# Expert logits from one side-by-side operand: eight matmuls a token tile instead of twelve

## The chip, the cores and the metric

The kernel runs on one core of a Trainium2 chip. The core has TensorE (PE; its weight loads are listed as PEld), VectorE (DVE), ScalarE (ACT), GpSimd (POOL) and SyncE (SP, which issues most DMA transfers; its queue is listed as SPq). The metric is device time in microseconds (us), lower is better. Before the change the median of 3 runs is 1145.32 us (1145.3 to 1145.65).

## What is computed

The reference chains three parts. Cut to what matters:

```python
# 1. attention between 512 tokens and 32 state rows, 8 batches x 8 heads, both ways -> 4352 tokens x 512
# 2. first MLP
h = x @ w_in                       # 512 -> 2048
x = np.maximum(h, 0.0) ** 2 @ w_out
# 3. one of 8 experts a token
xn = x / (np.linalg.norm(x, axis=-1, keepdims=True) + 1e-06)
en = expert_emb / (np.linalg.norm(expert_emb, axis=-1, keepdims=True) + 1e-06)
logits = xn @ en.T / tau
expert_idx = np.argmax(logits, axis=1)
gate_w = softmax(logits)[token, expert_idx]
out[mask] = gate_w * (np.maximum(x[mask] @ w1[e], 0.0) @ w2[e])   # for each expert e
```

## The kernel before

All matmuls work on 16-bit floats. To keep the precision of 32 bits, each operand is a pair of 16-bit halves, high and low, and each product is three matmuls: high by high, high by low, low by high.

The tokens are 34 tiles of 128. The first MLP takes two tiles (256 tokens) at a time, called u = 0 to 16: `up1` makes the hidden layer in 8 chunks (L1167 to L1169, or L1174 to L1176 for the last u, whose tokens come from the state side), `hidden` squares the ReLU on ScalarE (L1130, L1136) and splits it on VectorE into g_h and g_l (L1139, L1141), and `down1` multiplies by w_out (L1219 to L1221, four groups of 12 matmuls a tile). Each tile then goes through `route_tile`: ScalarE squares it for the norm (L1006), VectorE makes a scale, ScalarE and VectorE split it into halves (L308, L303), SP issues a DMA that transposes the halves into the tile xr (L1017), TensorE makes the 8 logits from xr and the expert embeddings (L1025 to L1028), and VectorE copies them out of PSUM (L1031). There is one buffer for xr. Four tiles together go through `route_group` (L1052 to L1105), a chain of small VectorE instructions that picks the expert, counts tokens and writes records to memory.

Beside this, `experts` prepares the expert weights: each is loaded in 1 MB pieces (stage, xx, wo_t), squared on ScalarE (L936), summed on VectorE (L872) and on TensorE by one small matmul (L878) for its scale, then converted into halves (L308 on ScalarE, L303 on VectorE, into he) and stored to w_d in memory (L325). There are 64 conversions of 1024 columns and two stores each. When all are stored, four 2 MB loads (L1436) bring the first experts' halves back; they also need the list of which expert comes first (`list_of`, whose small matmuls are L1255 and L1343). The expert MLP then runs 70 half steps on gathered tokens (L1527 to L1529, L1552).

Each engine runs its instructions in the order in which the program lists them. That order is made when the program is built, by the class `Plan`: each piece of work is a generator that yields an engine and a booked duration, and the planner lets the piece go next whose start is earliest, with a priority to break ties. A booking on TensorE for k matmuls of n columns is `pe(k, n)`: k times the larger of 4 ns and n x 0.4163 ns. A changed booking thus can change who goes next everywhere behind it. The order is fixed by then: where the chip's times differ from the bookings, nothing is corrected.

Of the kernel before, what the change touches and what calls it, by code (L numbers as in the profile page):

```python
# [11 lines left out]
F16 = mybir.dt.float16  # L12
# [3 lines left out]
ALU = mybir.AluOpType  # L16
X = mybir.AxisListType.X
# [5 lines left out]
NE, FE = 8, 1024  # L23
# [187 lines left out]
def act(n):  # L211
    return "act", 0.1 + 0.83e-3 * n
# [10 lines left out]
def tiny(k):  # L223
    return "dve", TINY * k


def pe(k, n):
    return "pe", k * max(0.004, n * 0.4163e-3)
# [3 lines left out]
def moe_kernel(  # L232
# [24 lines left out]
    const = ctx.enter_context(tc.tile_pool(name="const", bufs=1))  # L257
# [18 lines left out]
    mm = nc.tensor.matmul  # L276
    V = nc.vector
# [3 lines left out]
    def pow2(s, inv, v, K):  # L281

        m = small.tile([128, 4], F32, name="p2m")[:, :v.shape[1]]
        V.tensor_scalar(out=m.bitcast(I32), in0=v.bitcast(I32), scalar1=0x7F000000, scalar2=1,
                        op0=ALU.bitwise_and, op1=ALU.logical_shift_right)
        V.tensor_scalar(out=s.bitcast(I32), in0=m.bitcast(I32), scalar1=-1.0, scalar2=float(K << 23),
                        op0=ALU.mult, op1=ALU.add)
        V.tensor_scalar(out=inv.bitcast(I32), in0=m.bitcast(I32), scalar1=float((254 - K) << 23), scalar2=None,
                        op0=ALU.add)
# [15 lines left out]
    def split(hi, lo, src, scale, n):  # L305

        yield act(n)
        nc.scalar.activation(out=hi, in_=src, func=AF.Copy, scale=scale)  # L308
        yield dve(n)
        split_lo(lo, src, scale, hi)  # L310
# [46 lines left out]
    ise = const.tile([128, 2 * NE], F32, name="ise")  # L357
    u1 = const.tile([128, NT], F32, name="u1")
    itau = const.tile([128, 1], F32, name="itau")
    en_h = const.tile([128, 4, NE], F16, name="en_h")  # L360
    en_l = const.tile([128, 4, NE], F16, name="en_l")
    cum = const.tile([128, NT + 1, NE], F16, name="cum")
    nc.gpsimd.memset(cum[:, 0, :], 0.0)

# [15 lines left out]
    def ev(*key):  # L380
        return evs.setdefault(key, Ev(plan))
# [619 lines left out]
    def route_tile(i, ps, k_h, rc, st):  # L1001

        j = i % 4
        rc = rc.bitcast(F16)
        yield act(600)
        nc.scalar.activation(out=rc[:, 0:512].bitcast(BF16), in_=ps, func=AF.Square, accum_out=st["f2"][:, j:j + 1])  # L1006
        yield tiny(4)
        f2 = st["f2"][:, j:j + 1]
        V.tensor_scalar(out=f2, in0=f2, scalar1=FLOOR, scalar2=None, op0=ALU.max)  # L1009
        s2 = small.tile([128, 1], F32, name="s2")  # L1010
        pow2(s2, st["is2"][:, j:j + 1], f2, 204)
        yield from split(rc[:, 0:512], rc[:, 512:1024], ps, s2, 600)
        d_slots.release(k_h)
        yield xr_slots
        yield "sp", 0.06
        xr = mg.tile([128, 8, 128], F16, name="xr", bufs=XR)
        nc.sync.dma_start_transpose(xr, rc[:, 0:1024])  # L1017
        plan.cur[2] = plan.dma(1 << 18) + 1.0
        yield ev("en")
        at = plan.now()  # L1020
        yield t_slots
        plan.cur[2] = max(at, plan.now())
        pl = ps_t.tile([128, 512], F32, name="t")
        yield pe(12, NE)
        for k in range(4):  # L1025
            mm(pl[:, 0:NE], lhsT=xr[:, k, :], rhs=en_h[:, k, :], start=k == 0, stop=False)
            mm(pl[:, 0:NE], lhsT=xr[:, k, :], rhs=en_l[:, k, :], start=False, stop=False)
            mm(pl[:, 0:NE], lhsT=xr[:, 4 + k, :], rhs=en_h[:, k, :], start=False, stop=k == 3)  # L1028
        xr_slots.release()
        yield tiny(1)  # L1030
        V.tensor_copy(st["lg"][:, j, :], pl[:, 0:NE])  # L1031
        t_slots.release()
        ev("lg", i).set()

# [149 lines left out]
    def down1():  # L1184
        for u in range(NU):
            g = u // 2
            for j in range(2):
# [35 lines left out]
                if i % 4 == 0:  # L1223
                    plan.add(group_unscale(g), 1)
                plan.add(route_tile(i, ps, k_h, recs[-1], st), 2 if g < B else 0)
                if i % 4 == m - 1:
                    plan.add(route_group(4 * g, m, recs, k_r, st), 2 if g < B else 0)
# [447 lines left out]
```

## Time and profile before

| what | value |
|---|---|
| median of 3 runs | 1145.32 us |
| the profiled execution | 1157.43 us |
| its span, first to last instruction | 1155.6 us |
| mean granted TensorE clock | 0.959 of full speed |
| PE busy | 1032.8 us, 89% |
| DVE busy | 708.0 us, 61% |
| ACT busy | 583.3 us, 50% |
| POOL busy | 126.2 us, 11% |

The span is the time from the first to the last instruction of one profiled execution. Busy shares are averages over stages that differ: the page's second part cuts the span into 40 slices of 28.9 us, with one digit for tenths busy.

```profile
PE   2255899999999999999999999699999999999995
DVE  6998877968869878688696784356422222222221
ACT  6689777776776977677777873111111111101110
PEclk8579799999999999999999999899999999999998
```

The first four slices load weights and start the attention, the 25th and 26th are the passage from the first MLP to the expert MLP.

### The profile page before, as it was taken

What the parts mean: (1) busy time and instruction counts of PE and PEld (TensorE: products, weight loads), DVE (VectorE), ACT (ScalarE), POOL (GpSimd) and SP (SyncE); (2) the same over time, 40 slices, a digit from 0 to 9 for tenths busy, and PEclk for the clock granted to TensorE, in tenths of its full rate; (3) what the DMA queues carried; (4) which work ended last, traced back from release to release, by engine and by line L of the source; (5) the groups of instructions that cost most, each with busy time, mean ns of one, the idle gap of its engine ahead of it and who ended that gap; (6) DMA issues with size and microseconds to landing.
All of it is one profiled execution on the core that took longest, in us unless ns stands there. A gap on an engine that the chain in (4) does not pass through costs nothing. (4 is left out here: it accounts for less than half of the span.)

```text
span 1155.6 us, 26458 instructions
## 1 busy us (share of the span) xinstructions
PE 1032.8 (89%) x10707; PEld 665.2 (58%) x10707; DVE 708.0 (61%) x1838; ACT 583.3 (50%) x959; POOL 126.2 (11%) x149
## 2 busy tenths in 40 slices
PE   2255899999999999999999999699999999999995
PEld 1134356555555555565555666377776777767773
DVE  6998877968869878688696784356422222222221
ACT  6689777776776977677777873111111111101110
POOL 0200000200100201002001010212121211211201
PEclk8579799999999999999999999899999999999998
DMA  9345466566685685656736676634696777685690
GB/s 354 112 151 128 151 159 211 105 193 145 183 223 125 209 238 157 189 117 183 238 71 229 205 232 273 167 92 93 209 297 173 204 213 206 185 250 155 179 295 28
DMA packets 160546, 211.77 MB, mean 183 GB/s; under 512 B 112226, under 2 KB 113506, under 8 KB 155171
## 3 DMA queue, kind: packets, MB, share of 16 engines
q1 hardware_dynamic: 152098, 182.94, 55.5%
q0 software_dynamic: 8320, 27.08, 7.2%
q8 instruction: 86, 1.41, 0.5%
q14 instruction: 42, 0.34, 0.1%
HBM read 257.92 MB, written 51.68 MB: 268 GB/s over the span
## 5 line engine op out<-in xcount | busy, mean ns | idle before, releaser
L1219 PE MATMUL d<-wo_t,g_h 128*128 128x512 f16 x544 | 209.7, 386 | 3.6 <-DVE g_h L1139 1.4
L1221 PE MATMUL d<-wo_t,g_l 128*128 128x512 f16 x544 | 209.3, 385 | 1.8 <-DVE l L1063 1.8
L1220 PE MATMUL d<-wo_t,g_h 128*128 128x512 f16 x544 | 209.5, 385 | 1.2 <-DVE wo_t L303 1.2
L1486 ACT ACTIVATE r<-u 128x512 f32<-128x512 f32 x70 | 41.8, 597 | 324.5 <-PE u L1529 300.0
L1167 PE MATMUL u<-aT,sw 128*128 128x256 f16 x512 | 141.5, 276 | 25.3 <-ACT r L1130 22.5
L1169 PE MATMUL u<-aT,sw 128*128 128x256 f16 x512 | 141.4, 276 | 0.9 <-DVE sw L303 0.9
L1168 PE MATMUL u<-aT,sw 128*128 128x256 f16 x512 | 141.3, 276 | 0.0
L1130 ACT ACTIVATE r<-u,cg 128x512 f32<-128x512 f32 x136 | 93.0, 684 | 72.9 <-PE u L1176 35.4
L1489 DVE CAST hh<-r 128x512 f16<-128x512 f32 x70 | 30.4, 434 | 136.5 <-ACT r L1486 134.4
L1105 POOL DMA_INDIRECT rec_d<-rec,pi x34 | 37.8, 1112 | 576.6 <-DVE f L1009 175.7
L1141 DVE TENSOR_TENSOR g_l<-r,g_h 128x512 f16<-128x512 f32 x136 | 93.3, 687 | 6.5 <-ACT r L1136 5.1
L1500 DVE TENSOR_SCALAR o<-d,rec,wo_t 128x512 f32<-128x512 f32 x35 | 28.3, 810 | 108.9 <-PE d L1552 99.2
L1221 PEld LDWEIGHTS <-g_l 128*128 128x128 f16 x544 | 53.9, 99 | 70.2 <-issue 5.3
L1552 PEld LDWEIGHTS <-hh 128*128 128x128 f16 (+1 forms) x688 | 54.7, 102 | 56.9 <-issue 0.4
L1136 ACT ACTIVATE r<-r 128x512 f32<-128x512 f32 x136 | 85.6, 629 | 1.9
L1219 PEld LDWEIGHTS <-g_h 128*128 128x128 f16 x544 | 54.2, 100 | 55.9 <-issue 5.7
L1220 PEld LDWEIGHTS <-g_h 128*128 128x128 f16 x544 | 53.8, 99 | 53.5 <-issue 5.0
L1139 DVE CAST g_h<-r 128x512 f16<-128x512 f32 x120 | 50.9, 424 | 47.8 <-ACT r L1136 44.7
L1527 PE MATMUL u<-xes,stage 128*128 128x128 f16 x448 | 75.9, 219 | 0.0
L1529 PE MATMUL u<-xes,stage 128*128 128x128 f16 x448 | 75.9, 219 | 0.0
L1528 PE MATMUL u<-xes,stage 128*128 128x128 f16 x448 | 75.9, 219 | 0.0
L1168 PEld LDWEIGHTS <-sw 128*128 128x128 f16 x512 | 50.6, 99 | 37.6 <-issue 26.5
(334 smaller groups left out, 2682.3 us busy)
## 6 DMA issues: line engine op xcount, KB each, us to landing
w_d<-he SPq DMA_DIRECT2D x128, 256.0 KB
wo_t<-w_d SPq DMA_DIRECT2D x16, 2048.0 KB
stage<-w_d SPq DMA_DIRECT2D x14, 2048.0 KB
he<-w_d SPq DMA_DIRECT2D x14, 2048.0 KB
xx<-w_d SPq DMA_DIRECT2D x13, 2048.0 KB
sw<-w_d SPq DMA_DIRECT2D x13, 2048.0 KB
stage<-in_w_dram SPq DMA_DIRECT2D x20, 1024.0 KB
g_h<-w_d SPq DMA_DIRECT2D x8, 2048.0 KB
```

Of the source, the lines that this page charges most:

```text
L1130: nc.scalar.activation(out=r, in_=ps, func=AF.Relu, scale=cg[:, g:g + 1])
L1136: nc.scalar.activation(out=r, in_=r, func=AF.Square)
L1141: V.tensor_tensor(out=gl, in0=r, in1=gh, op=ALU.subtract)
L1167: mm(o, lhsT=hl[:, i, 0, fs], rhs=aT[:, i, :], start=i == 0, stop=False)
L1168: mm(o, lhsT=hl[:, i, 0, fs], rhs=aT[:, 2 + i, :], start=False, stop=False)
L1169: mm(o, lhsT=hl[:, i, 1, fs], rhs=aT[:, i, :], start=False, stop=i == 1)
L1219: mm(ps, lhsT=g_h[:, f, ts], rhs=w[:, 0, :], start=f == 0, stop=False)
L1220: mm(ps, lhsT=g_h[:, f, ts], rhs=w[:, 1, :], start=False, stop=False)
L1221: mm(ps, lhsT=g_l[:, f, ts], rhs=w[:, 0, :], start=False, stop=f == KF - 1)
L1527: mm(p[:, j, xs], lhsT=w[:, 0, k, fs], rhs=xe[:, k, xs], start=k == 0, stop=False)
L1528: mm(p[:, j, xs], lhsT=w[:, 0, k, fs], rhs=xe[:, 4 + k, xs], start=False, stop=False)
L1529: mm(p[:, j, xs], lhsT=w[:, 1, k, fs], rhs=xe[:, k, xs], start=False, stop=k == 3)
```

## The change

The two halves of the expert embeddings, 8 columns each, are put into one tile of 16 columns. The high half of the tokens is multiplied by all 16 at once; the low half of the tokens by the first 8 as before. Two sums of 8 columns stand in PSUM, and the instruction that takes them out adds them: a reduction over two elements in place of a copy. The booking for the planner falls from 12 matmuls to 8.

```diff
-    en_h = const.tile([128, 4, NE], F16, name="en_h")
-    en_l = const.tile([128, 4, NE], F16, name="en_l")
+    en = const.tile([128, 4, 2 * NE], F16, name="en")
+    en_h, en_l = en[:, :, 0:NE], en[:, :, NE:2 * NE]
...
         pl = ps_t.tile([128, 512], F32, name="t")
-        yield pe(12, NE)
+        yield pe(8, NE)
         for k in range(4):
-            mm(pl[:, 0:NE], lhsT=xr[:, k, :], rhs=en_h[:, k, :], start=k == 0, stop=False)
-            mm(pl[:, 0:NE], lhsT=xr[:, k, :], rhs=en_l[:, k, :], start=False, stop=False)
+            mm(pl[:, 0:2 * NE], lhsT=xr[:, k, :], rhs=en[:, k, :], start=k == 0, stop=False)
             mm(pl[:, 0:NE], lhsT=xr[:, 4 + k, :], rhs=en_h[:, k, :], start=False, stop=k == 3)
         xr_slots.release()
         yield tiny(1)
-        V.tensor_copy(st["lg"][:, j, :], pl[:, 0:NE])
+        V.tensor_reduce(out=st["lg"][:, j, :], in_=pl[:, 0:2 * NE].rearrange("p (a e) -> p e a", a=2), axis=X, op=ALU.add)
```

From the logits on, all line numbers of the changed kernel are smaller by one (L1130 of before is L1129, and so on). The order of instructions changes on all engines. Three places follow.

On ScalarE, at the end of the expert conversions (L308 into he): in the program before, the square of the 31st tile (L1006) stands ahead of the last conversion.

```order
L308 ACTIVATE he<-xx,se 128x1024 x2
L1130 ACTIVATE r<-u,cg 128x512
L1136 ACTIVATE r<-r 128x512
L1006 ACTIVATE rec_8505,f_8056<-d 128x512
L308 ACTIVATE he<-xx,se 128x1024
L308 ACTIVATE rec_8505<-d,s_8835 128x512
```

The same place on ScalarE in the changed program, from the ReLU ahead of the last conversion to the 31st tile's square:

```order
L1129 ACTIVATE r<-u,cg 128x512
L308 ACTIVATE he<-xx,se 128x1024
L1135 ACTIVATE r<-r 128x512
L1129 ACTIVATE r<-u,cg 128x512
L1135 ACTIVATE r<-r 128x512
L1129 ACTIVATE r<-u,cg 128x512
L1135 ACTIVATE r<-r 128x512
L1006 ACTIVATE rec_8402,f_7926<-d 128x512
```

The last conversion moved ahead of the square, with two chunks of the hidden layer between them.

On TensorE, at the last of the scale matmuls (L878): before, it stands among the last u's first chunk, which comes behind tile 30 of the first MLP.

```order
L1175 MATMUL u<-x_l,wi_h 128x256
L1176 LDWEIGHTS wi_l
L1176 MATMUL u<-x_h,wi_l 128x256
L878 MATMUL t<-fv,one_95 128x1
L1026 LDWEIGHTS xr
```

And on TensorE in the changed program, where the down matmuls are the third of four groups of the 30th tile:

```order
L1219 MATMUL d<-wo_t,g_h 128x512
L1220 LDWEIGHTS g_l
L1220 MATMUL d<-wo_t,g_l 128x512
L878 MATMUL t<-fv,one_95 128x1
L1166 LDWEIGHTS sw
```

The scale matmul moved ahead of the end of the 30th tile and of the last chunks of the 16th u.

On VectorE, in the second half of the routing chain of the last four full tiles (from L1062, which marks the best expert, to L1076, which counts; L1139 and L1141 split a chunk of the hidden layer), before:

```order
L1062 TENSOR_TENSOR eq<-l_9207,lm 128x32
L1063 TENSOR_TENSOR l_9207<-l_9207,lm 128x32
L1141 TENSOR_TENSOR g_l<-r,g_h 128x2x256
L1072 TENSOR_TENSOR eq<-eq,cs 128x32
L1073 TENSOR_REDUCE em<-eq 128x4
L1074 TENSOR_TENSOR oh<-cs,em 128x32
L1076 TENSOR_TENSOR cum<-cum,oh 128x8 x4
L684 TENSOR_TENSOR gt<-icg,ismin 128x1
```

And there in the changed program:

```order
L1061 TENSOR_TENSOR eq<-l_9009,lm 128x32
L1062 TENSOR_TENSOR l_9009<-l_9009,lm 128x32
L1140 TENSOR_TENSOR g_l<-r,g_h 128x2x256
L1138 CAST g_h<-r 128x2x256
L1071 TENSOR_TENSOR eq<-eq,cs 128x32
L1072 TENSOR_REDUCE em<-eq 128x4
L1073 TENSOR_TENSOR oh<-cs,em 128x32
L1075 TENSOR_TENSOR cum<-cum,oh 128x8 x4
L1140 TENSOR_TENSOR g_l<-r,g_h 128x2x256
L1138 CAST g_h<-r 128x2x256
L1140 TENSOR_TENSOR g_l<-r,g_h 128x2x256
L684 TENSOR_TENSOR gt<-icg,ismin 128x1
```

Before, the last chunk's split ends inside the chain; in the changed program two more chunks are split in and behind it, so the chain stands two chunks earlier.

## Rows read from the trace of the kernel before

**Rows 1.** Stages (us from start): busy us and count by engine, PE clock, DMA share, GB/s.

```profile
725.00:752.00 27.00, 16.89 (x107) 8.88 (x105) 9.03 (x49) 4.24 (x8) 6.28 (x7) 0.81 0.62 140
752.00:1128.00 376.00, 371.40 (x5102) 272.17 (x5101) 126.11 (x328) 42.14 (x72) 68.90 (x68) 1.00 0.68 196
```

**Rows 2.** PE's timeline, waits: start us, us, instruction, [idle before <- what ended it].

```profile
609.87 0.27 PE L1167 MATMUL u<-aT,sw 128*128 128x256 f16 x1 [2.58 <-ACT r L1130]
...
732.63 0.19 PE L1026 MATMUL t<-en_h,xr 128*128 128x8 f16 x1 [6.85 <-DMA xr<-rec]
...
744.39 0.39 PE L1219 MATMUL d<-wo_t,g_h 128*128 128x512 f16 x1 [1.42 <-DVE g_h L1139]
...
746.83 0.61 PE L1221 MATMUL d<-wo_t,g_l 128*128 128x512 f16 x1 [1.84 <-DVE l L1063]
```

**Rows 3.** PE's timeline, starts of groups of twelve, at full and at reduced clock.

```profile
698.18 0.38 PE L1219 MATMUL d<-wo_t,g_h 128*128 128x512 f16 x1
...
700.77 0.27 PE L1174 MATMUL u<-x_h,wi_h 128*128 128x256 f16 x1
...
702.08 0.38 PE L1219 MATMUL d<-wo_t,g_h 128*128 128x512 f16 x1
...
732.97 0.59 PE L1219 MATMUL d<-wo_t,g_h 128*128 128x512 f16 x1
...
737.28 0.27 PE L1174 MATMUL u<-x_h,wi_h 128*128 128x256 f16 x1
...
751.92 0.18 PE L1083 MATMUL t<-oh,cs 128*128 128x32 f16 x1
```

**Rows 4.** Lines of PE: busy us, mean ns | idle before, releaser.

```profile
L1026 PE MATMUL t<-en_h,xr 128*128 128x8 f16 x136 | 13.6, 168 | 9.5 <-DMA xr<-rec 9.5
```

**Rows 5.** PE's timeline, a logits block and 48 matmuls of 64 columns, with the next.

```profile
158.56 0.17 PE L1026 MATMUL t<-en_h,xr 128*128 128x8 f16 x1
...
158.86 0.27 PE L1167 MATMUL u<-aT,sw 128*128 128x256 f16 x1
...
573.80 0.19 PE L484 MATMUL S<-sth,xx 128*128 128x64 f16 x1
...
575.20 0.27 PE L1167 MATMUL u<-aT,sw 128*128 128x256 f16 x1
```

**Rows 6.** Lines of DVE: the copy of the logits and a small reduction.

```profile
L1031 DVE COPY lg<-t 128x8 f32<-128x8 f32 x34 | 5.5, 161 | 18.2 <-PE t L1028 11.3 <-remote 6.6
...
L1097 DVE TENSOR_REDUCE gs<-ex 128x4 f32<-128x32 f32 (+1 forms) x9 | 1.6, 176 | 0.0
```

**Rows 7.** Timelines of DVE and PE: sums of squares and the scale matmuls behind them.

```profile
625.67 0.16 DVE L872 TENSOR_REDUCE fv<-pacc 128x1 f32<-128x4 f32 x1 [1.22 <-ACT pjk L936]
...
629.81 0.17 PE L878 MATMUL t<-fv,one 128*128 128x1 f32 x1
...
639.86 0.16 DVE L872 TENSOR_REDUCE fv<-pacc 128x1 f32<-128x4 f32 x1 [0.91 <-ACT pjk L936]
...
643.22 0.17 PE L878 MATMUL t<-fv,one 128*128 128x1 f32 x1
```

**Rows 8.** ACT's timeline at the last conversion.

```profile
701.02 0.60 ACT L1006 ACTIVATE rec<-d 128x512 bf16<-128x512 f32 x1 [1.59 <-PE d L1221]
...
701.60 1.14 ACT L308 ACTIVATE he<-xx,se 128x1024 f16<-128x1024 f32 x1
```

**Rows 9.** SP's queue: last stores, first weight load, the transposes behind the four loads.

```profile
691.69 12.73 SPq L325 DMA_DIRECT2D w_d<-he  x8
706.47 0.37 SPq L1436 DMA_DIRECT2D stage<-w_d  x1
...
712.72 21.65 SPq L1017 DMA_TRANSPOSE xr<-rec  x2
```

**Rows 10.** Timelines: PE behind tile 30, DVE behind the list's matmuls.

```profile
676.75 0.27 PE L1167 MATMUL u<-aT,sw 128*128 128x256 f16 x1
...
696.75 0.17 DVE L1349 COPY wo_t<-t 128x6 f32<-128x6 f32 x1 [0.74 <-PE t L1343]
```

## The prediction

> **What bounds the kernel now.** I read the page's forty slices first. TensorE is nearly full from the seventh slice on, so from about 150 us its instructions, in their order, set the end, and a microsecond taken from it shortens the run if no wait takes its place. Next I read the stages: from 752 to 1128 us TensorE is busy 371.4 of 376 us, from 725 to 752 only 16.9 of 27 at a granted clock of 0.81 [rows 1]. Whatever delays or advances TensorE at 752 therefore arrives at the end nearly whole, and the place where time lies about is the passage from the first MLP to the expert MLP.
>
> Then the timeline of TensorE, for the waits in it. Between 550 and 752 us there are four of over a microsecond: 2.58 us for a ReLU on ScalarE, 6.85 us for a logits operand (xr) that a DMA turns, then 1.42 and 1.84 us for pieces of the hidden layer [rows 2]. After the 6.85 us the next twelve 512-column matmuls take from 732.97 to 737.28, 4.31 us, where the same twelve took 698.18 to 700.77, 2.59 us; the sixteen after the wait at 746.83 end at 751.92, 5.09 us where 16/12 of 2.59 is 3.45 [rows 2, 3]. These stretches ran in part at 1.2 instead of 2.4 GHz: 1.7 and 1.6 us. The passage so costs 6.85 + 1.42 + 1.84 + 1.7 + 1.6 = 13.4 us.
>
> **Part one: the matmuls and the way out of PSUM.** Line L1026 ran 136 times, and L1027 and L1028 as often: 34 tiles of 12 matmuls [rows 4]. One block starts at 158.56 and the next matmul at 158.86: 0.30 us, 25 ns each, although one record reads 168 ns; records overlap [rows 4, 5]. Four of the twelve go, and four of the other eight get 16 columns, which the trace doesn't show. Its bounds: 8 columns at 25 ns, and 64 columns, 48 of which run from 573.80 to 575.20, 29 ns [rows 5]. So eight cost 0.20 to 0.22 us; I take 25 ns, since 16 lies nearer to 8 than to 64. Saved: 34 x 0.10 = 3.4 us (2.7 at the other bound), 2.8 of it in the 28 tiles up to 677 us and 0.6 behind. On VectorE the copy of 161 ns becomes a reduction of 16 elements to 8; a small one of 32 to 4 takes 176 ns, the copy's 161 is the other end [rows 6]. 34 x 15 ns is 0.5 us at most, on an engine that waits often in these stretches: nothing on the path. Uncovered it would be 0.5 us.
>
> The Trainium skill ("TensorE: Matmul & The Clock Gate", section "Wait — 56ns, not 53.3ns?") says that the spacing of matmuls never falls under about 25 ns however few columns there are; by it the saving is 3.4 us, by the 64-column row 2.7. The 25 ns of 8 columns agree with it.
>
> **Part two: what moves.** The planner books 8 x 4 ns instead of 12 x 4 ns for the block, and from there on ranks threads differently. With line numbers aligned, TensorE's order differs in a short stretch near 290 us and in a long one from about 535 to 770 us; behind that it is the same. Three moves matter.
>
> First, the small matmuls that finish an expert weight's scale (L878) stand earlier. The last four before were at 629.81, 643.22 and two later; the sums of squares they read were ready 3.98 and 3.20 us before the first two [rows 7]. At the first, the change has 24 fewer 512-column matmuls ahead (5.2 us at 2.59 per 12), 30 fewer of 256 columns (3.3 us at 1.31 per 12), one state block and one logits block fewer (about 1 us), and 2.4 us less from shorter logits: 12 us earlier [rows 3]. The squares come only about 4 us of ScalarE's work earlier. 12 - 4 - 4 leaves a wait of 4. At the second, TensorE is 13.9 us earlier by the same counting, less the 4 just lost, the squares 4.4: 13.9 - 4 - 4.4 - 3.2 leaves 2.3. At the last two it comes out near 0.5 and none. That is 6.8 us of new waits, the upper end. The lower end is below nothing: the wait of 2.58 us, with slow clock behind it as behind the others (1.6), may go, since the order there is new: -4.2 [rows 2]. I take +4.8, nearer to the counted end. Behind each L878 all of TensorE is queued.
>
> Second, the last conversions of expert weights. Before, the final one (he<-xx at 701.60) stood behind the routing square (L1006 at 701.02) that waited for the 31st tile of the first MLP; the four 2 MB weight loads followed at 706.47, and the transposes of the operand for logits 31 were queued behind them on SP at 712.72; the operand arrived 26.1 us after the first load's issue, at 732.6 [rows 2, 8, 9]. Now all conversions stand ahead of that square, behind a ReLU whose matmuls end 11.9 us of TensorE work after tile 30, which ended at 676.75 [rows 10]: 688.6. Conversion, its low half, and the store (2.8 us from ScalarE's start to the end of SP's last store at 704.42, 2.05 us more to the load [rows 8, 9]) would allow loads near 694. But they also need the list of experts, whose matmul L1343 ended just before VectorE's copy at 696.75 [rows 10]; in the new order it ends at about 693.3, then about 1.4 us on VectorE behind the conversions, and the reads on SP: I take first load at 697.3, arrival 26.1 later, 723.4. The bounds are 694 and 706.5.
>
> Third, the logits of tiles 31 and 32 stand earlier: ahead of logits 31 there are 12 fewer 512-column and 48 fewer 256-column matmuls (2.6 + 5.2 = 7.8 us). TensorE reaches them at 676.75 + 40.1 us of counted work = 716.9 and waits 6.5 us, about as before. It leaves 9.2 us earlier (723.4 for 732.6) with 7.8 us more to do: -1.4. But now the routing chain on VectorE runs beside the 48 matmuls, and 12 matmuls stand between the last of these and the first that needs the last hidden pieces; so the 1.42 and 1.84 us and the second 1.6 us of slow clock go. What is late next is the gathered expert tokens; four groups of 2.59 us cover them. Together -1.4 - 4.9 = -6.3.
>
> **The sum** for the profiled execution (span 1155.6 of 1157.43 us): -2.8 + 4.8 - 6.3 - 0.6 = -4.9. The median of the runs is 12.1 us shorter than that execution; nothing shows where, so I subtract it there: 1145.32 - 4.9 = 1140.4 us. The likeliest case reaches from 1133 to 1143.
>
> **Rivals.** (a) Only the matmuls count, and moved waits cancel: 1145.3 - 3.4 = 1141.9, or 1142.6 at the other bound. For it: before and after hold the same work. Against: the passage is visibly re-ordered. (b) The shortened blocks are given back: TensorE waits for ScalarE in places, and time saved ahead of such a wait may only lengthen it: 1145.3. For it: the 2.58 us is such a wait. Against: ScalarE and VectorE take their inputs from TensorE and come earlier with it. (c) Slower. The weight loads don't come earlier, since conversions lag on VectorE or the stores on SP: then they start at 706.5 as before, logits 31 run at 732.6, and the 7.8 us of work that now stands behind is added: +7.8 - 4.9 = +2.9; with new scale waits of 6.8, less 3.4: +6.3, 1151.6. It decides from a first load later than about 702 us. For it: VectorE has low halves of 1.28 us to do just there; a matmul that is moved ahead of its input stops all behind it. Here the Trainium skill speaks against the change (same page, section "Step-by-step: what each phase is for"): matmuls keep program order, only weight loads are pulled ahead; the 6.85 us with ready work behind agree. Against (c): the conversions precede the square in ScalarE's order, so their old gate is gone. That the change doesn't do what it says is excluded: the new program issues 136 matmuls fewer.
>
> **How the numbers follow.** Forecast 0.55, (a) 0.17, (b) 0.11, (c) 0.17. What a measurement tells from no change is 0.2%, 2.3 us. Most of the forecast and two thirds of (a) are faster by more: 0.49 + 0.11 = 0.60; (b), the rest of (a) and some of the forecast are within: 0.22; (c) and a little are slower: 0.18. With load bounds 694 and 706.5 and scale waits -4.2 to 6.8, the range is 1133 to 1149.
>
> **What would show it.** Right: logits blocks of 0.20 us; L878 with waits of some us between 610 and 660; first weight load near 697; one wait of about 6 us at logits 31, none of size behind it until the expert MLP. Wrong: loads at 702 or later, or a wait in the passage at another place, such as the scale matmuls of the last expert or the list matmul; or TensorE waits near 290 us that weren't there.

## The result and the profile after

The changed kernel takes **1137.0 us** (median of 6 runs, 1135.8 to 1140.4) against 1145.5 us for the kernel before beside it (6 runs): ratio **0.9907, 95% interval [0.988, 0.9933]**. The forecast was 1140.4 us. Direction and place were right; two of its terms were not the right size. Two runs of the controls below (1567 and 2734 us) were far longer than all others of their kernel and are left out of the medians.

The two profiled executions, 1157.43 and 1135.79 us, lie further apart than the medians. To read them I set three marks on TensorE: the start of the logits of tile 28 (the last that has nearly the same work ahead of it in both orders: six 256-column matmuls fewer after, 0.7 us), the first second-projection of the expert MLP (the matmuls of `hh` and `hl`), and the last of the 34 blocks in which these come. Between the first two lies what I call the passage; behind the second mark both kernels do the same.

| kernel profiled | logits 28 | passage | first to last block |
|---|---|---|---|
| before | 652.5 | 118.6 | 360.9 |
| before again | 644.5 | 118.4 | 355.4 |
| after | 644.3 | 111.1 | 354.9 |
| after again | 650.7 | 109.3 | 354.6 |

The two ends of the passage in before, and its end in after (the start of logits 28 there, 644.32, is shown further down):

```profile
652.47 0.17 PE L1026 MATMUL t<-en_h,xr 128*128 128x8 f16 x1
...
771.06 0.59 PE L1552 MATMUL d<-he,hh 128*128 128x512 f16 x2
```

```profile
755.37 0.59 PE L1551 MATMUL d<-he,hh 128*128 128x512 f16 x2
```

The passage is the difference that repeats: 7.3 to 9.3 us. The start of logits 28 scatters by 6 to 8 us between executions of one kernel. The last column has two values, about 355 and about 361 us, which I come to at the end. So of the 21.6 us between the two profiles shown, 7.5 are the passage, 6 are behind it, and 8 ahead of it lie within that scatter.

The stage of the passage after, in the same columns as [rows 1]: 27 us around the wait, and the 376 us behind.

```profile
709.00:736.00 27.00, 22.94 (x151) 14.37 (x151) 11.76 (x58) 6.87 (x12) 5.84 (x7) 0.87 0.39 82
736.00:1112.00 376.00, 374.18 (x5178) 275.79 (x5178) 126.88 (x328) 43.27 (x74) 71.29 (x69) 1.00 0.70 199
```

TensorE was busy 16.9 of 27 us at a granted clock of 0.81; now it is 22.9 at 0.87. Its waits (start, duration, instruction, idle before and what ended it), which answer [rows 2]:

```profile
609.06 0.41 PE L549 MATMUL S<-wi_h,sth 64*32 64x512 f16 x8 [1.51 <-DVE fv L872]
...
622.29 0.38 PE L878 MATMUL t<-fv,one 128*128 128x1 f32 x2 [0.59 <-DVE fv L872]
...
638.80 0.27 PE L1166 MATMUL u<-aT,sw 128*128 128x256 f16 x1 [0.96 <-ACT r L1129]
...
640.93 0.27 PE L1166 MATMUL u<-aT,sw 128*128 128x256 f16 x1 [0.66 <-ACT r L1129]
...
713.28 0.19 PE L1026 MATMUL t<-en,xr 128*128 128x16 f16 x1 [4.06 <-DMA xr<-rec]
713.51 0.37 PE L1173 MATMUL u<-x_h,wi_h 128*128 128x256 f16 x1
...
716.03 0.63 PE L1218 MATMUL d<-wo_t,g_h 128*128 128x512 f16 x1
...
720.28 0.27 PE L1173 MATMUL u<-x_h,wi_h 128*128 128x256 f16 x1
```

One wait is left in the passage, 4.06 us for the logits operand of tile 31; the 1.42 and 1.84 us are gone. Behind it the granted clock is 0.50 (1.2 GHz) from 713.5 to 719.2 us and 1.00 from 720.3: twelve 256-column matmuls take 2.52 us (713.51 to 716.03) instead of 1.31, the next twelve of 512 columns 4.25 (to 720.28) instead of 2.59 [rows 3].

SP's queue (start, duration), which answers [rows 9]:

```profile
677.09 7.31 SPq L325 DMA_DIRECT2D w_d<-he  x6
689.32 0.37 SPq L1435 DMA_DIRECT2D stage<-w_d  x1
691.41 0.35 SPq L1435 DMA_DIRECT2D he<-w_d  x1
693.28 0.34 SPq L1435 DMA_DIRECT2D xx<-w_d  x1
695.12 0.34 SPq L1435 DMA_DIRECT2D sw<-w_d  x1
695.57 20.40 SPq L1017 DMA_TRANSPOSE xr<-rec  x2
```

Tile 30 ends at 668.89, so the first load starts 20.4 us behind it; before it was 29.7 [rows 9, 10]. The transposes still stand behind all four loads.

The logits block and the way out of PSUM (timeline of TensorE: first matmul of the block, first behind it; then the lines of TensorE and VectorE with busy us and mean ns), which answer [rows 4 to 6]:

```profile
644.32 0.17 PE L1026 MATMUL t<-en,xr 128*128 128x16 f16 x1
...
644.52 0.27 PE L1166 MATMUL u<-aT,sw 128*128 128x256 f16 x1
```

```profile
L1026 PE MATMUL t<-en,xr 128*128 128x16 f16 x136 | 11.1, 171 | 6.0 <-DMA xr<-rec 5.9
L1027 PE MATMUL t<-en,xr 128*128 128x8 f16 x136 | 10.8, 166 | 0.0
...
L1030 DVE TENSOR_REDUCE lg<-t 128x8 f32<-128x16 f32 x34 | 5.7, 169 | 18.7 <-PE t L1027 18.6
```

Eight matmuls take 0.20 us: a matmul of 16 columns costs as much as one of 8. The reduction takes 169 ns, 8 more than the copy, 0.3 us over all 34.

### The profile page after: what moved, and what is told of

Read it like the earlier page. It is cut to its first block, busy times and chain, and to the rows that moved or that the text cites. A ratio compares the mean times of both kernels' runs of the same rounds, so it can differ in the third digit from the quotient of the medians.

```text
span 1133.9 us, 26183 instructions
## 1 busy us (share of the span) xinstructions
PE 1020.8 (90%) x10571; PEld 659.3 (58%) x10571; DVE 706.8 (62%) x1838; ACT 583.2 (51%) x959; POOL 127.3 (11%) x149
## 5 line engine op out<-in xcount | busy, mean ns | idle before, releaser
L1166 PE MATMUL u<-aT,sw 128*128 128x256 f16 x512 | 140.7, 275 | 22.9 <-ACT r L1129 20.4
L1129 ACT ACTIVATE r<-u,cg 128x512 f32<-128x512 f32 x136 | 92.7, 682 | 59.5 <-PE u L1168 27.0
```

What stands on the lines that cost most here:

```text
L1129: nc.scalar.activation(out=r, in_=ps, func=AF.Relu, scale=cg[:, g:g + 1])
L1166: mm(o, lhsT=hl[:, i, 0, fs], rhs=aT[:, i, :], start=i == 0, stop=False)
```

## The experiments

The planner's booking sets the order and can be chosen apart from what a block contains. So the change can be cut into its two parts, without any other edit. In the traces TensorE, ScalarE and VectorE of the first two kernels below run the same sequence of instructions, but for the blocks themselves, as before and as after.

**Shorter blocks in the old order.**

```diff
-        yield pe(8, NE)
+        yield pe(12, NE)      # in the changed kernel: its 8 matmuls, the order of before
```

> Eight matmuls and the reduction as in the change, but the planner's booking left at 12, so that every engine keeps the order of before. Theory (the shorter blocks give 34 x 0.10 = 3.4 us, the new order the rest of the 8.5 us): about 1142, ratio 0.997, and the wait at logits 31 stays near 6 us, with waits of 1 to 2 us behind it. Rival 1 (only the matmuls count): about 1137, ratio 0.9926. Rival 2 (shorter blocks are given back in later waits, the order does all): about 1145.4, ratio 1.000.

Measured: 1155.7 us against 1156.2 on this chip, ratio 0.9993 [0.9972, 1.0015]. The passage is 118.0 us, with the old waits:

```profile
726.87 0.19 PE L1026 MATMUL t<-en,xr 128*128 128x16 f16 x1 [5.76 <-DMA xr<-rec]
738.16 0.39 PE L1218 MATMUL d<-wo_t,g_h 128*128 128x512 f16 x1 [1.44 <-DVE rL L1054]
740.62 0.61 PE L1220 MATMUL d<-wo_t,g_l 128*128 128x512 f16 x1 [1.84 <-DVE l L1062]
```

The blocks alone give 0.8 us, with an interval that leaves between 3.2 gained and 1.7 lost. The full 3.4 is just outside it.

**The new order with the old blocks.**

```diff
-        yield pe(12, NE)
+        yield pe(8, NE)       # in the kernel before: its 12 matmuls and the copy, the order of the change
```

> Twelve matmuls and the copy as before, but the booking set to 8, so that every engine has the order of the changed kernel. Theory (shorter blocks 3.4, order the rest): about 1140.4, ratio 0.9955, first expert weight load 20 us behind the end of tile 30 instead of 30, one wait at logits 31. Rival 1 (only the matmuls count): 1145.4, ratio 1.000. Rival 2 (the order does all): about 1137, ratio 0.9926.

Measured on the same chip: 1144.8 us, ratio 0.9895 [0.9868, 0.9923], with 12 matmuls a block. The passage is 112.3 us and has one wait:

```profile
719.75 0.19 PE L1026 MATMUL t<-en_h,xr 128*128 128x8 f16 x1 [5.84 <-DMA xr<-rec]
```

The order alone gives as much as the whole change did, and the two intervals of this pair are apart. The passages of the pair differ by 5.7 us, the medians by 11; where the rest lies these two profiles don't show.

**The transpose ahead of half of the loads.** If the remaining wait is the queue of four loads on SP, letting the transpose of tile 31's operand stand behind two of them should remove it. The edit holds two of the loads back until that transpose is issued.

```diff
         nc.sync.dma_start_transpose(xr, rc[:, 0:1024])
+        if i == 30:
+            ev("xr31").set()
...
                     yield ev("attention")
+                    if sides_of(t)[0] == 1:
+                        yield ev("xr31")
```

> The changed kernel with one move on SP's queue: the transpose for logits 31 is issued behind the first two of the four 2 MB expert weight loads instead of behind all four; all else keeps its order. Theory (the wait of 4.06 us at logits 31 is the queue of four loads, and the slow clock behind it, 2.9 us, comes from the wait): the operand arrives some 10 us earlier, the wait and the slow clock go, about 7 us: 1130, ratio 0.987 to the kernel before. Rival (the operand's own chain, from tile 31 through ScalarE and VectorE, or the transpose among other transfers, is what is late, or the later loads now hold up the expert MLP): same time as the changed kernel, 1137, ratio 0.9926, or a new wait at the first expert steps.

Measured: 1138.7 us, ratio 0.9846 [0.9818, 0.9874], better than the kernel before and the new order with the old blocks (1144.8) on this chip, and by its ratio better than the changed kernel on the others (0.9907, and 0.9929 and 0.9879 below). The passage is 103.5 us, and no wait of 0.3 us or more is left in it behind 655 us. SP's queue:

```profile
692.47 0.37 SPq L1439 DMA_DIRECT2D stage<-w_d  x1
694.56 0.35 SPq L1439 DMA_DIRECT2D he<-w_d  x1
695.77 4.10 SPq L1017 DMA_TRANSPOSE xr<-rec  x1
701.38 0.90 SPq L1439 DMA_DIRECT2D xx<-w_d  x1
704.26 0.34 SPq L1439 DMA_DIRECT2D sw<-w_d  x1
712.58 1.27 SPq L1017 DMA_TRANSPOSE xr<-rec  x1
```

The transpose is issued 3.3 us behind the first load, where it was 6.3, and with two loads ahead of it instead of four.

**Controls on a second chip.** The two kernels once more, unchanged.

> The kernel before once more, as if it were a changed one: a control. Every theory expects ratio 1.000; what it differs by shows how far two medians of the same kernel lie apart here. Its second profile should show again four waits in the passage or just ahead of it (about 6 us at logits 31, 1.4 and 1.8 us behind it) if these belong to the order and not to one execution.

Measured: 1146.8 us (11 runs), ratio 1.0007 [0.9983, 1.0032]. Three of the four waits come again (6.87 us at logits 31, 1.42 and 1.84 behind it); the 2.58 us doesn't.

> The changed kernel once more, beside the others of this call. Theory 1 (now: the order gives nearly all, the shorter blocks 0 to 3 us): ratio 0.989 to 0.991 to before. Rival (the shorter blocks are worth their 3.4 us on top of the order's 0.9895): 0.9865.

Measured: 1138.8 us against 1146.1, ratio 0.9929 [0.9906, 0.9953], a little less gained than expected; the rival's 0.9865 is outside. Their profiles are the second and fourth row of the table of marks. The first load starts at 695.60 and the operand's wait ends at 719.41, 23.8 us later, as in the profile of after (24.0).

**Longer blocks.** To see what share of a block's length reaches the end, the opposite of the change, in a size that can be measured: 24 extra matmuls of 8 columns a tile (0.6 us), into a part of PSUM that nobody reads. The order is that of after.

```diff
         yield pe(8, NE)
+        for k in range(24):
+            mm(pl[:, 64:64 + NE], lhsT=xr[:, k % 8, :], rhs=en_h[:, k % 4, :], start=True, stop=True)
```

> The changed kernel with 24 more matmuls of 8 columns in every logits block, into columns of the PSUM buffer that nothing reads; the order of all else is that of the changed kernel. At 25 ns each that is 34 x 0.6 = 20.4 us more on TensorE. Theory 1 (TensorE sets the pace, a block's length passes on to the end): 17 to 20 us over the changed kernel of this call, ratio to it about 1.017; then the 3.4 us of the change should pass on as well. Rival 2 (a block's length is taken up by the waits behind it): under 8 us over it, ratio under 1.007.

Measured: 1151.2 us, ratio 1.0058 [1.0035, 1.0081]. Of 20.4 us put in, 12.4 come out by the medians and 14.8 by the ratios: 61 to 73%, between the two expectations; the intervals of the two ratios leave 11 to 19 us. In the profiles the start of logits 28 is 3.3 us later than in after again and 9.7 later than in after, for 16.2 us put in ahead of it; the passage is 4.7 to 6.4 us longer, for 4.2 put in. As far as these profiles tell, what is lost is lost ahead of logits 28. The waits of TensorE from 158 to 655 us for the squared ReLU on ScalarE stand in the row of the line that waits (shape and count | busy us, mean ns | idle before in us, and by releaser). Here it is in before again, in after again and in this kernel, all on one chip:

```profile
L1167 PE MATMUL u<-aT,sw 128*128 128x256 f16 x428 | 117.0, 273 | 11.0 <-ACT r L1130 10.8
```

```profile
L1166 PE MATMUL u<-aT,sw 128*128 128x256 f16 x416 | 114.1, 274 | 14.3 <-ACT r L1129 14.3
```

```profile
L1168 PE MATMUL u<-aT,sw 128*128 128x256 f16 x411 | 112.1, 273 | 6.4 <-ACT r L1131 6.4
```

With 28 blocks longer by 0.6 us, 16.8 us in this stretch, these waits fall from 14.3 to 6.4. Whether they rise with 28 blocks shorter by 0.1 us isn't shown. Over the profiles the same wait reads 15.0, 10.8, 11.6 and 11.7 us in the four with 12 matmuls (mean 12.3), and 13.2, 14.3, 13.9, 13.0, 13.5, 15.2 and 7.7 in the seven with 8 (mean 13.0). The two executions of the kernel before lie 4.2 us apart, and the 7.7 belongs to the kernel of the next paragraph, which has another order:

```profile
L1166 PE MATMUL u<-aT,sw 128*128 128x256 f16 x424 | 115.7, 273 | 8.0 <-ACT r L1129 7.7
```

So an order alone can also take these waits out, and the fall to 6.4 us counts only against the profiles of its own order (11.6 to 14.3).

**Another booking.** With 4 in place of 8 the planner makes a third order; the blocks are those of after.

```diff
-        yield pe(8, NE)
+        yield pe(4, NE)
```

> The changed kernel with the booking at 4 instead of 8: same instructions, another order. In it the last conversion of expert weights stands two places behind the square of tile 31 (as before the change, even later), and logits 31 stand ahead of 36 more 512-column and 60 more 256-column matmuls than before (14 us of work). Theory 1 (the passage decides: loads as late as before, logits 31 earlier in the order): TensorE waits some 15 to 20 us at logits 31, and the kernel is slower than before by about 5 to 10 us, ratio 1.004 to 1.009. Rival 3 (what helped is any order in which the middle is different, or the shorter booking): ratio 0.98 to 0.995.

Measured: 1142.7 us, ratio 0.9971 [0.9954, 0.9988]; I had expected a slower kernel, and the expectation failed. I had read the orders of TensorE and ScalarE, but not that of SP. There the loads are late as expected, but tile 31's transpose stands ahead of them, and only one is behind:

```profile
698.27 1.24 SPq L1017 DMA_TRANSPOSE xr<-rec  x1
...
706.22 0.37 SPq L1435 DMA_DIRECT2D stage<-w_d  x1
...
713.85 9.91 SPq L1017 DMA_TRANSPOSE xr<-rec  x1
```

The wait moved to the next tile (5.17 us at 731.12), with 1.33 and 1.97 us behind it. The passage is 112.6 us, as in the new order with 12 matmuls (112.3): in these two profiles it matters less which tile waits than that one stands behind the four loads.

**The split in both orders, and with both blocks.** Four kernels on a third chip: the old order with the split (8 matmuls), the new order with the split again, the same with the 12 matmuls and the copy, and the changed kernel as control.

```diff
-        yield pe(8, NE)
+        yield pe(12, NE)      # in the split kernel above: the order of before, but for the split
```

> The changed blocks (8 matmuls) in the order of before, with the one other edit that the transpose for the last half tile may start behind two of the four weight loads. Theory 1 (the wait at logits 31 comes from the queue of four loads on SP, whatever the order of TensorE): the wait of 5.8 to 6.9 us at logits 31 and the 1.6 us of slow clock behind it go, so the stretch from logits 28 to the first second-projection is 110 to 111 us against 118.0, and the ratio to the kernel before is 0.990 to 0.994. Rival (the wait belongs to the order, and splitting the loads only moves it to the first experts' weights): stretch 117 to 118.5 us, ratio 0.998 to 1.002.

Measured: 1151.1 us against 1158.9, ratio 0.9921 [0.9889, 0.9952], where the old order without the split had 0.9993. The wait of 5.8 to 6.9 us at logits 31 is gone and the passage is 113.4 us, less gained than the 110 to 111 expected: smaller waits stand at other places in it, two of them for the operands of the next tiles. In this kernel the logits of tiles 31 and 32 also stand ahead of twelve 256-column matmuls (1.3 us) that stood ahead of them before, so TensorE's order isn't quite the old one; the wait of 1.86 us is at the second of these.

```profile
736.57 0.18 PE L1028 MATMUL t<-en,xr 128*128 128x16 f16 x1 [1.86 <-DMA xr<-rec]
742.92 0.39 PE L1222 MATMUL d<-wo_t,g_l 128*128 128x512 f16 x1 [1.26 <-DVE g_l L1142]
...
754.75 0.18 PE L1028 MATMUL t<-en,xr 128*128 128x16 f16 x1 [1.21 <-DMA xr<-rec]
```

> The split loads in the order of the change once more, on the chip on which its partners run. Theory 1: 0.984 to 0.989 to the kernel before, and 5 to 9 us below the changed kernel beside it; no wait of TensorE over 0.3 us between logits 28 and the first second-projection. Rival (the first measurement was the chip's): 0.991 to 0.995, level with the changed kernel.

Measured: 1140.4 us, ratio 0.9819 [0.9783, 0.9856]; passage 103.7 us, again without a wait of 0.3 us or more behind 655 us. So the gain wasn't a matter of the chip of the first measurement.

```diff
-            mm(pl[:, 0:2 * NE], lhsT=xr[:, k, :], rhs=en[:, k, :], start=k == 0, stop=False)
+            mm(pl[:, 0:NE], lhsT=xr[:, k, :], rhs=en_h[:, k, :], start=k == 0, stop=False)
+            mm(pl[:, 0:NE], lhsT=xr[:, k, :], rhs=en_l[:, k, :], start=False, stop=False)
...
-        V.tensor_reduce(...)   # the split kernel above, with the blocks of before
+        V.tensor_copy(st["lg"][:, j, :], pl[:, 0:NE])
```

> Split loads and the order of the change, with the 12 matmuls and the copy of before: the partner of the run ahead of it, from which it differs in the logits blocks alone. Theory 1 (a shorter block is worth its time only where no transfer ends behind it; here none does): 2.5 to 3.4 us slower than its partner (34 blocks by 0.10 us). Rival (what a shorter block saves, the ReLU and the scales give back as waits everywhere): within 1 us of its partner.

Measured: 1140.2 us, ratio 0.9826 [0.9789, 0.9864], level with its partner, where my theory had wanted 2.5 to 3.4 us more. Each median is known to some 4 us only, so this doesn't exclude a smaller gain from the blocks; it supports the rival. Its passage is 108.2 us, 4.5 longer than its partner's, with one wait of 2.41 us for tile 32's operand; the medians are level all the same, and one profile can't tell whether that wait comes with the longer blocks:

```profile
719.98 0.19 PE L1028 MATMUL t<-en_h,xr 128*128 128x8 f16 x1 [2.41 <-DMA xr<-rec]
```

> The changed kernel itself, as the control of this call. Both theories: 0.990 to 0.994 to the kernel before; the stretch from logits 28 to the first second-projection 109 to 111 us with a wait of about 4 us at logits 31.

Measured: 1147.4 us (6 runs), ratio 0.9879 [0.9837, 0.9922], a little better than expected. Its passage isn't known, so the wait expected in it is neither seen nor excluded. The split gives 7.0 us here (1147.4 to 1140.4; the two intervals overlap a little), and about 8 in the old order, by ratios from two chips (0.9993 and 0.9921).

## Why the prediction was right, and where it was not

**Part one, the blocks: length right, worth too high.** Eight matmuls take 0.20 us and the reduction hides, as predicted. But 3.4 us shorter was taken to be 3.4 us earlier. The blocks alone gave 0.8 +- 2.4 us, and beside their 12-matmul partner nothing; 61 to 73% of a larger length passes, which for 3.4 us would be 2.1 to 2.5. All three fit a worth between nothing and 2.5 us. What fails in the step is that I added up matmuls without the ReLU waits among them: rival (b), which I had priced for the whole change, is in part true of this half. How much of it is true of a block shortened by 0.1 us is below what these runs can tell.

**First move, the scale matmuls: the step with the largest error.** I took +4.8 us of new waits. After shows 0.59 us at a scale matmul there (622.29) and 1.51 us at a state block (609.06), both put down to the reduction L872; after again shows 0.87 us at that scale matmul. In all six profiles of the new order with 8 or 12 matmuls the scale matmul waits 0.58 to 0.87 us; the 1.51 us stands in one of them. The wait is there, at an eighth to under a half of the size. The part that was wrong is ScalarE's move ("only about 4 us"):

```profile
608.92 0.15 DVE L872 TENSOR_REDUCE fv<-pacc 128x1 f32<-128x4 f32 x1
...
622.08 0.16 DVE L872 TENSOR_REDUCE fv<-pacc 128x1 f32<-128x4 f32 x1 [0.33 <-ACT pjk L936]
```

```profile
609.83 0.38 PE L878 MATMUL t<-fv,one 128*128 128x1 f32 x2
```

Counted back from logits 28, the two scale matmuls stand 34.5 and 22.0 us ahead where they stood 22.7 and 9.3: 11.8 and 12.8 us earlier, near the 12 and 13.9 predicted. But their sums stand 35.4 and 22.2 us ahead where they stood 26.8 and 12.6 [rows 7]: 8.6 and 9.6 us earlier (9.4 and 10.0 in the second profiles), not 4 and 4.4. With these moves the same working leaves nothing at the first and about nothing at the second. The wait of 2.58 us that I had kept as a possible gain [rows 2] isn't in the second profile of the same kernel at that size (0.63 us): one execution's wait is not yet the kernel's.

**Second move, the loads: right.** Predicted 20.55 us behind tile 30, measured 20.4, in after and in after again. The path was right too: in after the profile puts SP's wait just ahead of the loads (3.1 us) down to VectorE's work on the list of experts. The operand came 24.0 us behind the first load instead of 26.1, which the single figure from one profile couldn't tell; in the seven profiles with both transposes behind four loads it was 23.8 to 26.2.

**Third move, the passage: right.** TensorE reached logits 31 at 709.22, 40.3 us behind tile 30 (predicted 40.1). The wait was 4.06 us, not 6.5, because the operand came earlier, and the slow clock behind it cost 2.9 us, not 1.7. The two waits behind it went, and the gathered tokens weren't late. Predicted -6.3 and -0.6; measured -7.3 to -9.3 in the passage.

Near 290 us, the short stretch with another order, nothing new stands: the ReLU waits from 297 to 303 us are 2.0 us in sum before and 1.9 after.

Together: instead of -2.8 + 4.8 - 6.9 the runs show about nothing ahead of logits 28 (no gain can be seen over the scatter) and -7 to -9 in the passage, in sum -8.5 by the medians. Two errors of the forecast had opposite signs, so that 1140.4 came within 3.4 us of 1137.0 is in part luck: the order was taken at -1.5 in all and is worth 6 to 12. How much of this each of the three moves gives is read from traces; no run takes them apart. The prediction could place nowhere the 12.1 us by which its profile lay above the median; the second profile of that kernel, 13.7 us shorter, has 7.9 of them ahead of logits 28, 5.5 behind the passage and 0.2 in it. The range doesn't follow from the bounds it names: loads at 694 and scale waits of -4.2 give 1128, loads at 706.5 and 6.8 give 1151.6, and why it was narrowed to 1133 to 1149 isn't said.

Rival (a), where the order cancels, is excluded by the pair of the first two experiments, and (c) by the first load, 20.4 us behind tile 30 (697.2 on the clock of before, where (c) wanted 702 or later). Neither the split nor the order shows what sets the time from 158 to 655 us; that 7.9 of 16.8 us put in there came out of ReLU waits points to ScalarE, which was not tried.

## What to carry to other kernels

When an edit also changes a planner's booking, build the order and the edit apart: two runs told what no trace could. Read the order of every queue that feeds a wait, the DMA queue first: to let one small transpose pass two large loads gave 7 us here, nearly as much as the whole change. Time taken from an engine counts for less than its length where its next waits are set by another engine.

## What was not expected of the hardware

From the first to the last block of second projections, work in which all kernels are alike, profiles took either 354 to 355 us (after, its repeat, before again, and the runs beside them on the second chip) or 360 to 362 (before as first shown, all profiles on the other two chips). The longer ones hold more short waits that nothing in the profile ends. TensorE's waits in this stretch (line, releaser, total us, times, longest) in before, and in after:

```profile
PE u L1528 <- issue: 2.2, 5, 0.5
PE u L1527 <- issue: 1.4, 3, 0.5
```

```profile
PE u L1526 <- issue: 1.7, 1, 1.7
```

These account for 2 of the 6 us. All 6 stand in eight of the 33 steps from one block to the next: 10.78 us each in after, but for one of 12.67, and 11.03 to 12.58 in before; the other 25 agree within 0.01 us. What sets these eight apart stays open. The chips differ by more in the medians (before: 1146.1 on the second, 1156.2 and 1158.9 on the others), so a gain of 8 us can be read only against the kernel before on the same chip.
